# Attention with a relative bias, then a squared-relu layer: v of two batches as fp32 by another queue, x turned by pairs, layer 1 begun with three of four pairs

## The chip, the cores and the metric

The kernel runs on one core of a Trainium2 chip. A core has five engines with their own instruction streams: TensorE (PE, matrix products; its weight loads are shown apart as PEld), VectorE (DVE), ScalarE (ACT), GpSimd (POOL) and SyncE (SP). Sixteen DMA engines move data; they are fed by queues, of which this kernel uses the software queue, issued by GpSimd, and hardware queues, issued by SyncE and ScalarE. The metric is device time in microseconds of one execution.

## The reference

For 8 batches, 8 heads, 576 positions and 64 channels it computes an attention whose bias depends on the distance alone, and puts the result, as 4608 tokens of 512 channels, through two layers with a squared relu between them:

```python
scores = scale * np.matmul(q, k.transpose(0, 1, 3, 2))
bias = bias_table[bucket]                     # bucket of |i - j|, constant from 128 on
attn = softmax(scores + bias.transpose(2, 0, 1)[None])
x = (attn @ v) -> [4608, 512]
h = np.maximum(x @ w_in, 0.0)                 # w_in [512, 2048]
out = h * h @ w_out                           # w_out [2048, 512]
```

All inputs and the output are fp32.

## The kernel before

Products run in fp16. The attention is cut into 32 pairs of heads (four to a batch). `load_six` and `load_rows` bring q and k of a pair into staging tiles `qs`, `ks`, `load_v_head`, `load_v` and `load_v_tail` bring v into `va` (keys 0 to 511) and `vm` (the last 64 keys). All these go by the software queue, which changes fp32 to fp16 on the way; only pair 0's q and k come as fp32 through SyncE's and ScalarE's queues, into a part of a tile `g` that layer 1 uses much later, and are cast by `cast_first` (L463 to L472).

`pair` does one pair. TensorE turns q and k (L608; batches 0 to 2, later batches by DMA), their evacuation L570 (ScalarE) or L572 (VectorE) gives `qt` and `kt`, and L635 spreads the last 64 rows into `qz`. L653 forms the scores of 128 keys for both heads, L702 those of the last keys, L677 those of the last queries. ScalarE takes exponentials of them into `pt` and `pm` (L664, L712, L687). The bias is a factor, exp(bias) from a table `tb_sb` (made by L353 and L365/L367, `tm_sb` by L374), that VectorE multiplies onto the band where it isn't constant (L745). Then L781 and L788 multiply by v in two parts, of three and of two tiles of 128 queries, into the one bank `pv`; a column of constants in v makes the sums, and L805 and L810 divide by them and write `x`.

`x_turn` (batches 0 to 2) is called once for a batch: for each of five tiles of queries it turns the four pairs' x by TensorE (L848) and copies the result into `xt`. Later batches do it by DMA (L826).

`layers` works on groups of 512 tokens: sixteen pieces of layer 1, each of four products of 512 columns (L1044), a relu (L1065 on ScalarE, L1067 on VectorE for the first groups), a square (L1075), and the pieces of layer 2 of the group before, in `second` (L962), which computes with seven products of halves in place of eight (L921 forms sums for it).

PSUM has two score banks pairs `st`, one bank `pv` and three banks `f` that all else shares.

Nothing of this is issued in the order of the text. `P.add` records each piece with its engines, an assumed duration, what it depends on, the buffers it uses, a due time and an earliest time; `Plan.schedule` places the pieces in a simulated order: each engine takes what can begin first, then what is due first. The instructions are then emitted in that order, and each engine executes its own in order. So an assumed duration or a due time changes the order of instructions, and nothing else. The constants at the top (L31 to L41) set due times: `LEAD`, `FAST` and `PERIOD` those of the pairs, `AHEAD` how early a pair may start, `G0` and `GP` those of the groups of layers, `ORDER` the sequence of loads, `QUIET` and `LATER` earliest times of the constant fills (L388), `EV` up to which pair evacuations are VectorE's alone.

The software queue's loads of v of batch 0 are issued after those of pairs 1 to 3 and one of w_in.

Of the kernel before, what the change touches and what calls it, by code (L numbers as in the profile page):

```python
# [25 lines left out]
GT = 512  # L26
# [4 lines left out]
PERIOD, LEAD, FAST, FASTN = 9600.0, 1600.0, 3000, 7  # L31
AHEAD, G0, GP = 20600.0, 54700.0, 35900.0
DT_X = 3
RELU_DVE = 2
NSTG, NQK, NPT, NV, NX, NGB, NRT, NY = 5, 4, 3, 3, 6, 2, 4, 4
QUIET, LATER = 5200.0, 8500.0
TAB, EV = 6400.0, 1
P_ORDER = "1 6 2 5 7 3 4"
P_LAST = "1 6 2 5 7 3 4"
SIX = 3  # L40
ORDER = "k0 i0 q0 q1 v i1 i2 o0 k1 o1 i3 o2 o3"  # L41
# [149 lines left out]
def kernel(  # L191
# [74 lines left out]
    def loader(eng_name, eng, out_, in_, packets, deps=(), bufs=(), due=0.0):  # L266

        lane = [Buf(r_lane)] if eng_name == "POOL" else []
        issue = P.add(
            {eng_name: 720.0 if eng_name == "POOL" else 600.0},  # L270
            lambda: io(eng.dma_start(out=out_(), in_=in_())),  # L271
            deps,
            list(bufs) + lane,
            due,
        )
        return P.add({"DMA": packets / 16}, None, [issue], list(bufs) + lane, due if lane else -1e9), issue
# [9 lines left out]
    def load(eng_name, eng, out_, in_, packets, deps=(), bufs=(), due=0.0):  # L286
        return loader(eng_name, eng, out_, in_, packets, deps, bufs, due)[0]
# [15 lines left out]
        128 * 27, due=0,  # L303
# [21 lines left out]
        {"PE": 250.0},  # L325
# [21 lines left out]
    for c in range(6):  # L347
# [11 lines left out]
        o = P.add({"PE": 16 * 55.0}, t_mm, [o_eb, l_oh], [t_b], LEAD + TAB, 0.0, "f")  # L359
# [27 lines left out]
    def fill(ap, value, ns, due, after, deps=()):  # L387
# [3 lines left out]
    z_fix = [[fill(zz[:, 0], 0.0, 150.0, 10, QUIET)], [fill(zz[:, 1:], 0.0, 300.0, 11, LATER)]]  # L391
    first = [
        fill(pt_sb[:, :, PW:], 1.0, 150.0, 20, LATER),
        fill(pm_sb[:, :, S:], 1.0, 150.0, 20, LATER),
# [11 lines left out]
        fill(stg[i][w][96:128, 512:640].bitcast(FP32), 0.0, 90.0, 40 + i, 25000.0)  # L406
# [56 lines left out]
    def cast_first(w):  # L463

        def cast(o):
            src, dst = first_f[0:96, ts(w, 768)], stg[b_stg[0].slot][w][0:96, :]
            if o.eng == "ACT":
                io(nc.scalar.activation(out=dst, in_=src, func=COPYF))
            else:
                io(nc.vector.tensor_copy(out=dst, in_=src))  # L470

        l_qk[0, w] = [one_of({"ACT": act(768), "DVE": dve(768, 2.0)}, cast, [l_first[w]], [b_stg[0]], -3.0)]  # L472

    def load_v_head(b, h):
        l = load(
            "POOL", nc.gpsimd,
            lambda: vas[b_v[b].slot][:, :, h, 0:64],
            const(v[b, h, 0:512, :].rearrange("(t p) d -> p t d", p=128)),
            512 * 34.5, v_fix[min(b, 1)], [b_v[b]], pdue(),
        )  # L480
        l_v.setdefault((b, h // 2), []).append(l)
# [12 lines left out]
    def load_v(b):  # L494
# [9 lines left out]
        load_v_tail(b)  # L504

# [22 lines left out]
    for hp in range(4):  # L528
# [5 lines left out]
        if hp == 2:  # L534
            load_v_tail(0)
        if hp >= 1:
            for h in range(2 * hp - 2, 2 * hp):
                load_v_head(0, h)
    for h in range(6, 8):
        load_v_head(0, h)  # L540
    for step in ORDER.split():
# [7 lines left out]
        else:  # L549
            load_v(1)  # L550
# [11 lines left out]
    xt_ready, x_last = {}, {}  # L562
# [17 lines left out]
    def pair(p):  # L580
# [5 lines left out]
        for w, dst in ((0, qts), (1, kts)):  # L586
# [14 lines left out]
            def tr(w=w, bank=bank):  # L601
                ps = g_ps[bank.slot].bitcast(FP16)
                t = stg[b_stg[p].slot][w]
                if b < SIX:
# [11 lines left out]

            o = P.add({"PE": 12 * 36.0 if b < SIX else 5 * mm(128)}, tr, l_qk[p, w] + [l_id], [bank, b_stg[p]], T - 3000, after, "c" if b < SIX else "f")

# [152 lines left out]
        for part, qt0, nq in ((0, 0, 3), (1, 3, 2)):  # L771
            bank = Buf(r_pv)

            def pv(qt0=qt0, nq=nq, bank=bank):
                ps = pv_ps[bank.slot][:, 0 : nq * 130].rearrange("p (t e d) -> p t e d", t=nq, e=2)
# [27 lines left out]
            def recip(nq=nq, bank=bank, rb=rb):  # L803
                ps = pv_ps[bank.slot][:, 0 : nq * 130].rearrange("p (t e d) -> p t e d", t=nq, e=2)
                io(nc.vector.reciprocal(out=rs[rb.slot][:, 0:nq], in_=ps[:, :, :, 64:65]))  # L805

            def norm(nq=nq, bank=bank, rb=rb, qt0=qt0):
# [289 lines left out]
    for b in range(B):  # L1097
        norms = [pair(4 * b + hp) for hp in range(4)]
        if b < DT_X:
            x_turn(b, norms)  # L1100
# [38 lines left out]
```

The softmax here doesn't subtract the row's maximum and nothing guards it: scores larger than these inputs give would overflow.

## Time and profile before

| | |
|---|---|
| time, median of 13 runs | 377.3 us (375.82 to 378.54) |
| the profiled execution | 377.51 us, its span 375.7 us |
| mean granted TensorE clock | 0.995 |
| busy: PE, DVE, ACT, POOL | 361.0, 268.8, 255.4, 178.8 us |
| software queue | 94496 packets, 18.07 MB, 62.7% of 16 engines' span |
| hardware queues of loads, stores and transposes | 51280 packets, 19.75 MB, 25.9% |
| first pv product; first product of layer 1 | 20.47 us; 40.65 us |

A profile is of one execution. Its span goes from the first to the last instruction; the execution's time also has what lies around it. Busy time of TensorE counts from a product's start to its modelled end, so that a busy TensorE is not one at its peak. A wait is put down to the engine whose event came last.

### The profile page before, as it was taken

How to read it: one execution, taken by the hardware profiler on the slowest of the kernel's cores; microseconds unless marked ns; L12 is line 12 of the kernel's file. 1: busy time of each engine (PE TensorE's matmuls, PEld its weight loads, DVE VectorE, ACT ScalarE, POOL GpSimd, SP SyncE). 2: the span in 40 equal slices, each digit the busy share in tenths (PEclk: the TensorE clock that was granted, in tenths of full speed). 3: DMA queues.
4: the chain of work that ended last, by engine and by line, in shares of the span. 5: the costliest groups of instructions: out<-in, count | busy, mean ns of one | idle time of the engine just before them, and what ended most of it. 6: DMA issues, size and time to landing. Idle time of an engine off the chain costs nothing.

```text
span 375.7 us, 10050 instructions
## 1 busy us (share of the span) xinstructions
PE 361.0 (96%) x4046; PEld 247.4 (66%) x4046; DVE 268.8 (72%) x612; ACT 255.4 (68%) x361; POOL 178.8 (48%) x318
## 2 busy tenths in 40 slices
PE   3888999999999999999999999999999999999996
PEld 2665546745778666687766765677577888556775
DVE  3987789998788586767685777757776683583653
ACT  4988889987667886866787778746885541564330
POOL 8877453889476582933768456754550000000000
PEclk9989999999999999999999999999999999999999
DMA  9999999799999799949999699899990222100103
GB/s 172 150 131 155 200 167 80 47 92 86 101 152 138 93 120 139 109 52 122 138 132 71 107 124 160 76 105 107 160 108 30 77 58 71 67 2 28 58 28 112
DMA packets 146163, 38.74 MB, mean 103 GB/s; under 512 B 128070, under 2 KB 146118, under 8 KB 146118
## 3 DMA queue, kind: packets, MB, share of 16 engines
q0 software_dynamic: 94496, 18.07, 62.7%
q1 hardware_dynamic: 51280, 19.75, 25.9%
q8 instruction: 31, 0.51, 0.6%
q10 hardware_dynamic: 342, 0.30, 0.3%
q14 instruction: 14, 0.11, 0.1%
HBM read 36.88 MB, written 9.44 MB: 123 GB/s over the span
## 4 chain that ended last, share of the span: by engine, by line
PE 90%; DVE 4%; ACT 3%; DMA 1%; issue 1%; ACTq 0%
PE f L1044 34%; PE f L962 29%; PE pv L788 10%; PE st L653 8%; PE pv L781 3%; PE st L702 2%; PE f L608 1%; PE st L677 1%; DMA g<-in_k_dram 1%; ACT pt L664 1%; ACT pt L687 1%; PE f L848 1%; DVE tb_sb L367 1%; DVE pt L745 1%; DVE kt L572 0%
## 5 line engine op out<-in xcount | busy, mean ns | idle before, releaser
L1044 PE MATMUL f<-xt,w_in_sb 128*128 128x512 f16 (+4 forms) x704 | 142.1, 341 | 0.0
L664 ACT ACTIVATE pt<-st 128x1024 f16<-128x1024 f32 x128 | 126.7, 1023 | 22.4 <-PE st L653 22.4
L1065 ACT ACTIVATE rt<-f 128x512 f16<-128x512 f32 x134 | 80.0, 598 | 62.0 <-PE f L1044 60.3
L1044 PEld LDWEIGHTS <-w_in_sb 128*128 128x128 f16 x704 | 62.6, 98 | 53.0 <-issue 10.8
L1075 DVE TENSOR_TENSOR g<-rt 128x512 f16<-128x512 f16 x144 | 60.6, 423 | 41.2 <-ACT rt L1065 40.1
L745 DVE TENSOR_TENSOR pt<-pt,tb_sb 128x1536 f16<-128x1536 f16 (+2 forms) x96 | 58.3, 622 | 10.4 <-ACT pt L664 10.1
L962 PEld LDWEIGHTS <-g 128*128 128x128 f16 x576 | 54.9, 98 | 15.4 <-issue 4.7
L788 PE MATMUL pv<-va,pt 128*128 128x65 f16 x1280 | 55.5, 194 | 0.1
L788 PEld LDWEIGHTS <-pt 128*128 128x128 f16 x1280 | 51.0, 98 | 3.1 <-issue 0.7
L271 POOL DMA_DIRECT2D qs<-in_q_dram x71 | 49.8, 719 | 2.0 <-DMA ks<-in_k_dram 0.9
L271 POOL DMA_DIRECT2D ks<-in_k_dram x71 | 50.0, 713 | 1.4 <-DMA kt<-ks 0.8
L962 PEld LDWEIGHTS <-s 128*128 128x128 f16 x432 | 40.6, 98 | 10.6 <-issue 3.4
L635 POOL COPY qz<-qt 64x64 f16<-64x64 f16 x53 | 15.6, 294 | 61.9 <-DMA qt<-qs 39.0
L989 DVE SCALAR_TENSOR_TENSOR y<-f,y 128x512 f32<-128x512 f32 (+1 forms) x47 | 31.3, 667 | 16.1 <-PE f L962 15.1
L653 PE MATMUL st<-qt,kt 64*128 64x512 f16 x256 | 40.4, 385 | 1.5 <-ACT pt L664 0.5
L635 POOL COPY qz<-kt 64x64 f16<-64x64 f16 x59 | 20.7, 351 | 36.3 <-DMA kt<-ks 22.9
L962 PE MATMUL f<-w_out_sb,s 128*128 128x256 f16 x288 | 36.6, 273 | 0.0
L962 PE MATMUL f<-wt,g 128*128 128x256 f16 x288 | 36.6, 273 | 0.0
L962 PE MATMUL f<-w_out_sb,g 128*128 128x256 f16 x288 | 36.2, 273 | 0.1
L781 PE MATMUL pv<-vm,pm 128*128 128x130 f16 x160 | 35.5, 222 | 0.5 <-DVE x L810 0.4
L810 DVE TENSOR_TENSOR x<-pv,r 128x384 f16<-128x384 f32 x64 | 31.3, 490 | 1.9
L271 POOL DMA_DIRECT2D va<-in_v_dram x36 | 30.8, 860 | 0.4 <-issue 0.2
(62 smaller groups left out, 306.8 us busy)
## 6 DMA issues: line engine op xcount, KB each, us to landing
out_dram<-y SPq DMA_DIRECT2D x34, 256.0 KB, 2.4
va<-in_v_dram POOLq DMA_DIRECT2D x28, 128.0 KB, 4.7
qs<-in_q_dram POOLq DMA_DIRECT2D x40, 64.0 KB, 3.3
ks<-in_k_dram POOLq DMA_DIRECT2D x40, 64.0 KB, 2.8
w_in_sb<-in_moe_w_in_dram POOLq DMA_DIRECT2D x4, 512.0 KB, 7.5
w_out_sb<-in_moe_w_out_dram POOLq DMA_DIRECT2D x4, 512.0 KB, 9.8
qs<-in_q_dram POOLq DMA_DIRECT2D x11, 144.0 KB, 5.1
ks<-in_k_dram POOLq DMA_DIRECT2D x11, 144.0 KB, 5.9
```

What stands on the lines that cost most here:

```text
L271: lambda: io(eng.dma_start(out=out_(), in_=in_())),
L635: io(eng.tensor_copy(out=dst[qb.slot][rw, rw], in_=src[qb.slot][rw, 512:576]))
L653: nc.tensor.matmul(sets_ps[st.slot][:, e, :], kt[rw, ts(jt, 128)], qt[rw, 0:512], start=True, stop=True,)
L664: nc.scalar.activation(out=p5(pts[pb.slot])[:, jt, :, 0:512], in_=sets_ps[st.slot], func=EXPF, scale=SCALE)
L745: io(nc.vector.tensor_tensor(out=a, in0=a, in1=t, op=MULT))
L781: nc.tensor.matmul(ps[:, i, :, :], pm[:, c : c + 128], vm[:, hp, :, 0:65], start=True, stop=False)
L788: nc.tensor.matmul(ps[:, i, e, :], pt[:, (2 * jt + e) * S + c : (2 * jt + e) * S + c + 128], va[:, jt, 2 * hp + e, 0:65], start=False, sto ...
L810: nc.vector.tensor_tensor(out=xs[xb.slot][:, qt0 : qt0 + nq, :].rearrange("p t (e d) -> p t e d", e=2), in0=ps[:, :, :, 0:64], in1=rs[rb.s ...
L962: nc.tensor.matmul(g_ps[bf.slot][:, ts(s_, HALF)], left(c, s_), right(c), start=(c == 0 and (s_ == 0 or apart) and i not in before), stop= ...
L1044: nc.tensor.matmul(g_ps[bank.slot][:, a:z], w_in_sb[:, kk, ts(nt, 128)], xt_sb[:, kk, c : c + z - a], start=(kk == 0), stop=(kk == 3),)
L1065: io(nc.scalar.activation(out=rts[rb.slot], in_=g_ps[bank.slot], func=RELUF))
L1075: nc.vector.tensor_tensor(out=gs[gb1.slot][:, nt, :], in0=rts[rb.slot], in1=rts[rb.slot], op=MULT)
```

## The change

v of batches 0 and 1 is fetched by `fetch_v` as fp32, six DMAs each on SyncE's queue, into the free part of the last `g` tile (`room_f`, used by batch 0 and then by batch 1), and GpSimd casts it into `va` and `vm`, six casts each. The software queue's loads with an order number above 6, which is all after those of pairs 1 to 3, are made dependent on the first two casts (`v_cast[0:GATE]`). Layer 1 of the group that writes that `g` tile waits for all casts.

Pair 0's q and k are cast into an order in which six transposes of 128 rows do what twelve of 64 did. For batch 0 the second part of pv goes to a bank `f` instead of `pv`. `x_turn` is called for a pair, not a batch: three and two transposes, each with one copy. In the first group, three pieces of layer 1 (`PRE`) are split: the products of three pairs first, and that of pair 3 after. Relus of three groups, not two, may be VectorE's.

Assumed durations and the constants change too, and with them the order on every engine. The constant fills get early earliest times, and evacuations of pairs 1 to 4 become VectorE's alone.

```diff
-PERIOD, LEAD, FAST, FASTN = 9600.0, 1600.0, 3000, 7
-AHEAD, G0, GP = 20600.0, 54700.0, 35900.0
+PERIOD, LEAD, FAST, FASTN = 9200.0, 1800.0, 3000, 8
+AHEAD, G0, GP = 25000, 51600.0, 44700.0
-RELU_DVE = 2
+RELU_DVE = 3
-QUIET, LATER = 5200.0, 8500.0
-TAB, EV = 6400.0, 1
-P_ORDER = "1 6 2 5 7 3 4"
+QUIET, LATER = 1300.0, 900.0
+TAB, EV = 7800.0, 5
+P_ORDER = "1 2 6 5 7 3 4"
-ORDER = "k0 i0 q0 q1 v i1 i2 o0 k1 o1 i3 o2 o3"
+PV_G, PRE, FILL = 1, 3, 0
+V0_AT, V1_AT, V1_LAT, GATE = 3000.0, 15000.0, 12000.0, 2
+ORDER = "i0 q0 k0 k1 q1 i1 o0 i2 o1 o2 i3 o3"
...
+        if eng_name == "POOL" and due > 6.0:
+            deps = list(deps) + v_cast[0:GATE]
...
-        fill(stg[i][w][96:128, 512:640].bitcast(FP32), 0.0, 90.0, 40 + i, 25000.0)
+        fill(stg[i][w][96:128, 512:640].bitcast(FP32), 0.0, 90.0, 40 + i, FILL)
...
-            src, dst = first_f[0:96, ts(w, 768)], stg[b_stg[0].slot][w][0:96, :]
+            src = first_f[0:96, ts(w, 768)].rearrange("p (e j d) -> p e j d", e=2, j=6)
+            dst = stg[b_stg[0].slot][w][0:96, :].rearrange("p (j e d) -> p e j d", e=2, j=6)
...
+    room_f = gs[NGB - 1].bitcast(FP32).rearrange("p t c -> p (t c)")[:, 1536:]
+    r_room = Ring(1)
+    def fetch_v(b):
+        rb = Buf(r_room)
+        for tt in range(4):
+            l = load(
+                "SP", nc.sync,
+                const(room_f[:, ts(tt, 512)].rearrange("p (h d) -> p h d", h=H)),
+                const(v[b, :, ts(tt, 128), :].transpose([1, 0, 2])),
+                1024 * 19, (), [rb], -0.5 + b, after=(V0_AT, V1_AT)[b], turn=6.5 + 3 * b,
+            )
+            o = P.add(
+                {"POOL": 780.0},
+                lambda tt=tt: io(
+                    nc.gpsimd.tensor_copy(
+                        out=vas[b_v[b].slot][:, tt, :, 0:64],
+                        in_=room_f[:, ts(tt, 512)].rearrange("p (h d) -> p h d", h=H),
+                    )
+                ),
+                [l] + v_fix[min(b, 1)], [rb, b_v[b]], -1.0, (0.0, V1_AT + V1_LAT)[b],
+            )
+            v_cast.append(o)
+            for hp in range(4):
+                l_v.setdefault((b, hp), []).append(o)
...
-        if hp == 2:
-            load_v_tail(0)
-        if hp >= 1:
-            for h in range(2 * hp - 2, 2 * hp):
-                load_v_head(0, h)
-    for h in range(6, 8):
-        load_v_head(0, h)
+    fetch_v(0)
+    fetch_v(1)
...
+                if p == 0:
+                    for j in range(6):
+                        io(nc.tensor.transpose(ps[:, ts(j, 96)], t[0:96, ts(j, 128)], id_sb[0:96, 0:96]))
...
-            bank = Buf(r_pv)
+            bank, home = (Buf(r_g), g_ps) if b == 0 and part and PV_G else (Buf(r_pv), pv_ps)
...
+        for part, qt0, nq in ((0, 0, 3), (1, 3, 2)):
             bank = Buf(r_g)
+            n = min(128 * nq, S - 128 * qt0)
...
+                for i in range(nq):
+                    io(nc.tensor.transpose(ps[:, ts(i, 128)], xs[xb.slot][:, qt0 + i, :], id_sb))
...
+                ahead = 3 if g == 0 and i < PRE else 0
+                o = None
+                if ahead:
+                    o = P.add(
+                        {"PE": ahead * mm(512)}, lambda f1=f1: f1(k1=3),
+                        [x for kk in range(ahead) for x in xt_pair[g, kk]] + [l_win[nt // 4]], [bank, gb1],
+                        due + i * 2000, 0.0, "f",
+                    )
...
+                    [o] + (v_cast if g == NGB - 1 else []) + xt_ready[g] + [l_win[nt // 4]], [bank, gb1], due + i * 2000, 0.0, "f"
...
+        for p in range(4 * b, 4 * b + 4):
+            norms = pair(p)
+            if b < DT_X:
+                x_turn(p, norms)
```

## The prediction

> **What bounds the kernel now.** I read the page's busy shares first, then busy time by stretches of 10 us, then the waits of TensorE, then the chain that ended last inside the first 45 us. From the page:
>
> ```profile
> PE 361.0 (96%) x4046; PEld 247.4 (66%) x4046; DVE 268.8 (72%) x612; ACT 255.4 (68%) x361; POOL 178.8 (48%) x318
> ```
>
> Busy time by stretch (PE, PE's weight loads, DVE, ACT, POOL, then the granted clock and DMA):
>
> ```profile
> 0.00:10.00 10.00, 4.12 (x66) 3.03 (x66) 3.96 (x17) 4.75 (x7) 8.19 (x17) 1.00 0.96 174
> 10.00:20.00 10.00, 8.15 (x166) 5.53 (x161) 9.64 (x26) 9.51 (x13) 9.26 (x17) 1.00 1.55 150
> 20.00:30.00 10.00, 9.42 (x180) 7.19 (x178) 8.19 (x29) 8.66 (x13) 7.41 (x14) 0.83 1.27 107
> 30.00:40.00 10.00, 7.82 (x142) 5.63 (x137) 7.09 (x19) 8.46 (x14) 7.33 (x14) 1.00 1.21 190
> 40.00:50.00 10.00, 10.00 (x109) 4.89 (x107) 7.21 (x16) 8.52 (x11) 1.48 (x3) 1.00 1.24 203
> ```
>
> From 40 us on TensorE is full; its idle time lies in the first 40 us (10.5 us, of which 5.9 is the wait for the first k), 0.4 at 361 us and 3 us at the end. So nothing but the first 40 us can give time back; later, only the amount of TensorE work and its order count. The waits of TensorE name the opening one:
>
> ```profile
> PE f L608 <- DVE ks L470: 5.9, 1, 5.9
> ```
>
> The chain inside the first 45 us (start, length, what) then goes over VectorE until the first attention product:
>
> ```profile
> 5.88 1.19 PE f L608 x24
> ...
> 9.11 0.38 DVE qz L388
> 9.48 0.21 DVE pt L388
> 9.69 0.21 DVE pm L388
> 9.90 0.06 issue
> 9.96 0.50 DVE vm L388
> 10.46 0.14 DVE va L388
> ...
> 20.80 0.39 PE pv L788 x7
> ```
>
> The memsets of L388 stand on it for 1.5 us, and first pv waits for the bands of pair 0. By 1-us stretches TensorE's granted clock is 0.50 to 0.71 from 21 to 25 us, after a stretch (18 to 20) in which it was 47% busy; pieces of eight pv products take 0.39 there and 0.24 at 28 us. From 32.6 to 37.2 TensorE waits for ScalarE (0.85, 0.32 and 0.36 us), and the last turn of x waits 0.57 us for its normalisation:
>
> ```profile
> 33.81 0.40 PE L702 MATMUL st<-qt,qz 128*128 128x288 f16 x2 [0.85 <-ACT pt L664]
> ...
> 39.72 0.45 PE L848 MATMUL f<-id_sb,x 128*128 128x128 f16 x5 [0.57 <-DVE x L810]
> ...
> 40.65 2.76 PE L1044 MATMUL f<-xt,w_in_sb 128*128 128x512 f16 x12
> ```
>
> **What the Trainium skill says.** "TensorE: Matmul & The Clock Gate", Part 1, has the array at half clock until it has been busy for a window of some 3.4 us, and again after too little work; the 0.50 at 22 us agrees. "DMA: Bandwidth & Descriptors", Queues, rings and completion order: each DMA engine takes packets in turn from the queues that have work, so a second queue takes share from the first; this trace has only the software queue loaded early, so no line shows it. "SBUF — State Buffer", Who interferes with whom: VectorE in its two-port modes and GpSimd lock each other out; GpSimd's 64x64 copies take 0.23 us at 7 to 13 us and 0.29 to 0.35 on average, which fits without proving it.
>
> **The change, part by part.** Instruction counts are from the two programs' orders, durations from the trace.
>
> *Opening.* Pair 0's 24 transposes (two halves each) become 12 of full width. 24 took 1.19 us, so 0.6 us less on the chain: -0.6. The cast before them writes strided; I keep its 0.56 us (if its rate halved, +0.4).
>
> *Memsets.* The fills, 3.1 us in sum with the ten staging ones at 25.6 us, now stand ahead of the first cast, where VectorE is idle from 1.0 to 5.27 us. They fit with 1 us to spare; were they not covered, each would delay the first cast. Off the chain: -1.5.
>
> *VectorE or ScalarE.* Before the first pv VectorE has two more evacuations of 128x576 (2 x 0.75) and six fewer qz copies (6 x 0.2, now GpSimd's): +0.3. Up to the first relu VectorE has, in all, 12 such evacuations instead of 7 (+3.75), four more qz copies (+0.9), two more pm bands (+0.5), more but smaller x copies (+0.3), less the memsets: about 3 us more than before, against 6.3 us that it was idle between 5 and 40. ScalarE has 18 exponentials instead of 20 (-2.06), one more each of L712 and L687 (+1.26), three evacuations fewer (-2.0): -2.8. TensorE has the same work up to there (about 22 us by columns in both, at the rate of the 56 products that take 12.09 us from 323 us on). ScalarE's relief goes against the 1.5 us that TensorE waited for it at 33 to 37: -1.2. Of VectorE's remaining 2.7 us extra, most falls in its idle time; 1.0 comes through: +1.0 (bounds 0 and 2.7).
>
> *x by pairs, layer 1 with three pairs.* Only the last pair's five transposes are left at the end, and three groups can start without pair 3. Before, the closing stretch 37.55 to 40.65 held 20 transposes with a wait of 0.57: -0.9 (bounds 0 and -1.5). The second pv part goes to another bank; its wait on the normalisation was only 0.4 us in all; counted as nothing.
>
> *v.* Eight 64 KB, four 128 KB and four 32 KB loads leave the software queue: GpSimd saves 16 issues of 0.63 to 0.86 us and gains twelve casts. A cast of 128x512 is not in the trace. Bounds: 0.23 us (a 64-wide copy's price) and 8 x 0.23 = 1.84; I take 0.8, near one element a cycle plus a fixed part, and 0.5 for the tails. Casts of batch 0 follow the qz copies, so from about 13 us: 4 x 0.8 + 2 x 0.5 + two load issues (1.4) + a qz copy = 5.9, done at 19. The first pv needs all six and came at 20.5, so they are hidden; at 1.84 they would end at 24 and cost 3.5. Queued behind them are the loads of pair 4's and later q and k, w_in and w_out. Pair 4's q is issued between the casts at about 16 and lands 5 us later, wanted at about 23. The casts of batch 1 hold back the third and fourth w_in until about 33 us; those land by some 49 (7.5 us each, in turn), wanted from 48 on: hidden with little left. On SP's queue nothing stands behind the v loads until the transposes of batch 3. The v packets are now, by an estimate from the queues' averages, 30.4 ns each (25.9% x 16 x 375.7 us over 51280 on the hardware queue) instead of 39.9 (62.7% over 94496): 9216 packets, 5.5 us less DMA time; not on the path by itself. But batch 0's 4608 packets, 8.8 us of all engines, now run beside the q and k of pairs 1 to 3. I take +0.3 (bounds 0 and +4).
>
> *Later.* After layer 1 begins TensorE goes through 392 runs of one kind instead of 368. Ten are x turns between other work, the rest mostly f1 and f2 by turns. A run of eight f2 products took 0.98 us after another kind and 0.87 after f1, so a turn costs up to 0.11 on each side: 10 x 0.08 on average: +0.8 (bounds 0 and 2.6). Relus of the third group may go to VectorE, which was 94 to 97% busy from 60 to 90 us; it is spread over more time, so nothing.
>
> Sum: -0.6 - 1.5 + 0.3 - 1.2 + 1.0 - 0.9 + 0.3 + 0.8 = -1.8. Profiled span 375.7, so 373.9; the profiled execution took 377.51, 1.8 more than its span, and the median is 377.3, 1.6 above the span. Forecast 375.5.
>
> **Rivals.** *Absorbed:* VectorE becomes the bound of the opening. With 30.6 us of work from 5.3 and its old 5 to 6 us of idle time it lets layer 1 begin at 41, as before; the start's gain is gone, the turns stay, memsets help: 376.9. For it: VectorE 96% busy from 10 to 20. Against: part of its idle time was waiting for ScalarE.
>
> *Slower:* v's packets take half of the DMA engines while pairs 2 and 3 load. The last of the six loads, issued at 4.55, landed about 6 us later; at half rate the 4.3 us (0.86 MB at 200 GB/s) that were left from 4.2 us on become 8.6, so it lands near 15. In the new order pair 3's q is turned ahead of pair 0's last score, at about 12 us. From that point each microsecond of lateness stops TensorE in order, 3 us, and its clock falls again, 1 us more: -1.8 - 0.3 + 4 = +1.9, so 379.2. Against: only the first two v loads are issued at once; the other four wait for SP's earlier transfers and start near 5 us.
>
> *More:* the clock doesn't drop at 21 us, since transposes and tables fill 16 to 20: another 1.8 us, and VectorE's extra is all hidden, 1.0: 372.7.
>
> **How the numbers follow.** Forecast 0.50 (own range 373.7 to 376.5), absorbed 0.20, slower 0.20, more 0.10. A change within 0.2% (376.5 to 378.1) can hardly be told from none. Faster: 0.50 + 0.10 + a tenth of absorbed, 0.62; same: most of absorbed, 0.17; slower: 0.20 and a tail of absorbed, 0.21. The range 372.0 to 379.0 leaves out about the upper half of the slower case and the lower half of the larger gain.
>
> **What would show it.** Right: memsets before 5.2 us and none after; first layer-1 product at 38 to 40 us (40.65 before); no TensorE wait over 0.3 us on ScalarE there; the casts on GpSimd under 1 us and over before the first pv. Wrong: TensorE waiting on a q or k load between 9 and 17 us; the first pv released by GpSimd; VectorE busy over 95% from 20 to 40 us with layer 1 at 41 or later; layer 1's third quarter waiting for w_in; more TensorE idle time past 50 us.

## The result and the profile after

The changed kernel takes 381.43 us (median of 11 runs, 379.77 to 384.96) against 377.37 (48 runs, 375.82 to 379.18) on the same chips: ratio 1.0128 [1.0108, 1.0149]. It is 4.1 us slower; I forecast 1.8 us faster. The eleven times fall into two groups, six from 379.77 to 381.43 us and five from 383.67 to 384.96, and the median is the edge of the lower one. The profiled execution took 385.19 us, just above the upper group, with a span of 383.4 and a clock of 0.991, so its sums below are larger than the median's loss, and no trace shows an execution of the lower group.

Busy shares, from the page of the kernel after:

```profile
PE 363.4 (95%) x4034; PEld 247.1 (64%) x4034; DVE 276.2 (72%) x628; ACT 250.2 (65%) x354; POOL 171.5 (45%) x314
```

Of the 7.7 us between the two spans, 5.3 are idle time of TensorE (383.4 - 363.4 = 20.0 against 375.7 - 361.0 = 14.7), and 2.4 are TensorE busy for longer, with twelve products fewer. The stretches of 10 us after show where (same columns as for before: PE, PEld, DVE, ACT, POOL, clock, DMA share, GB/s), and then the last of them before:

```profile
20.00:30.00 10.00, 8.13 (x156) 5.72 (x154) 8.97 (x25) 7.84 (x10) 6.41 (x11) 1.00 1.27 203
30.00:40.00 10.00, 9.03 (x194) 6.52 (x191) 9.11 (x28) 9.57 (x17) 2.35 (x5) 1.00 0.81 131
40.00:50.00 10.00, 5.50 (x19) 2.11 (x21) 3.43 (x10) 2.29 (x5) 7.35 (x15) 0.68 1.02 157
...
70.00:80.00 10.00, 8.45 (x182) 6.87 (x178) 9.80 (x25) 9.08 (x14) 8.17 (x21) 1.00 0.45 30
```

```profile
70.00:80.00 10.00, 9.85 (x121) 5.80 (x117) 9.68 (x24) 9.53 (x16) 8.62 (x17) 1.00 0.75 54
```

From 40 to 50 us, where TensorE had been full, it is idle for 4.5 us and then runs at a lower clock; and from 70 to 80, where before had 9.85, it is idle for 1.5 us while VectorE is 98% busy (97% before). GpSimd, 2.35 us busy in the stretch ahead, is the odd one. The waits of TensorE after name it:

```profile
PE f L648 <- DVE ks L478: 5.9, 1, 5.9
PE st L750 <- POOL qz L683: 4.4, 1, 4.4
```

The first is the wait for the first k, as before; the second is new. TensorE's timeline after shows what it does (start, length, what, and in brackets the idle time before and who ended it):

```profile
40.12 0.81 PE L1090 MATMUL f<-xt,w_in_sb 128*128 128x512 f16 x3
45.31 0.66 PE L750 MATMUL st<-qt,qz 128*128 128x288 f16 x2 [4.37 <-POOL qz L683]
45.76 0.63 PE L725 MATMUL st<-qz,kt 128*128 128x128 f16 x4
46.19 3.62 PE L1090 MATMUL f<-xt,w_in_sb 128*128 128x512 f16 x8
```

Layer 1 begins at 40.12 us, 0.5 earlier than before, and after three products TensorE stands at a score that needs a `qz`. Eight products of layer 1 then take 3.62 us; eight took 1.90 in the kernel before, at 43.88 us. The Trainium skill, "TensorE: Matmul & The Clock Gate", Part 1, has half clock again after too little work; twice 1.90 is 3.80, so this agrees, with a mean clock of 0.68 in this stretch. GpSimd's timeline after says why `qz` was late:

```profile
29.74 0.63 POOL L520 CAST va<-g 128x512 f16<-128x512 f32 x1 [1.79 <-DMA g<-in_v_dram]
35.65 0.62 POOL L520 CAST va<-g 128x512 f16<-128x512 f32 x1 [5.29 <-DMA g<-in_v_dram]
37.47 0.40 POOL L544 CAST vm<-g 64x256 f16<-64x256 f32 x1 [1.21 <-DMA g<-in_v_dram]
38.97 0.40 POOL L544 CAST vm<-g 64x256 f16<-64x256 f32 x1 [1.10 <-DMA g<-in_v_dram]
39.42 0.74 POOL L277 DMA_DIRECT2D w_in_sb<-in_moe_w_in_dram  x1
40.15 1.49 POOL L277 DMA_DIRECT2D w_out_sb<-in_moe_w_out_dram  x2
...
44.45 0.51 POOL L683 COPY qz<-qt 64x64 f16<-64x64 f16 x2
```

It stood for 9.4 us (1.79 + 5.29 + 1.21 + 1.10) at the casts of batch 1, each waiting for its own load; behind them were seven issues of loads, and only then the copies. The chain that ended last (start, length, what) goes back over the load to SyncE's queue:

```profile
18.67 0.41 POOL vm L544
19.09 6.86 SPq L277
...
26.04 12.81 DMA g<-in_v_dram
...
38.97 0.40 POOL vm L544
...
44.45 0.23 POOL qz L683
...
45.31 0.66 PE st L750 x2
```

Batch 1's v uses the same room as batch 0's, so each of its loads waits for the cast that empties its part. That delays them little: the first four were issued at 14.77, 15.75, 17.09 and 18.30 us, each right behind such a cast. What is late is their landing. The third and fourth ended the waits at 29.74 and 35.65 us above, so they landed more than 12 and 17 us after their issue. The fifth issue then held SyncE for 7 us, and the last load, issued behind it, took 12.81 us more. SyncE's timeline after, in short windows:

```profile
18.30 0.50 SPq L277 DMA_DIRECT2D g<-in_v_dram  x1
18.89 7.06 SPq L277 DMA_DIRECT2D g<-in_v_dram  x1
26.04 1.13 SPq L277 DMA_DIRECT2D g<-in_v_dram  x1
```

The page's list of DMA issues after (KB each, median us from issue to landing):

```profile
va<-in_v_dram POOLq DMA_DIRECT2D x24, 128.0 KB, 4.7
...
g<-in_v_dram SPq DMA_DIRECT2D x8, 256.0 KB, 9.6
w_in_sb<-in_moe_w_in_dram POOLq DMA_DIRECT2D x4, 512.0 KB, 9.2
w_out_sb<-in_moe_w_out_dram POOLq DMA_DIRECT2D x4, 512.0 KB, 11.3
```

The w loads, 7.5 and 9.8 us before, are slower too. The Trainium skill, "DMA: Bandwidth & Descriptors", Queues, rings and completion order, has each DMA engine take packets in turn from the queues that have work. That fits the slow landings of v, but no run isolates it: of the eight w loads only three were issued while v was still on its way, the other five from 39.42 us on.

### The profile page after: what moved, and what is told of

Read it like the earlier page. It is cut to its first block, busy times and chain, and to the rows that moved or that the text cites. A ratio compares the mean times of both kernels' runs of the same rounds, so it can differ in the third digit from the quotient of the medians.

```text
span 383.4 us, 10056 instructions
## 1 busy us (share of the span) xinstructions
PE 363.4 (95%) x4034; PEld 247.1 (64%) x4034; DVE 276.2 (72%) x628; ACT 250.2 (65%) x354; POOL 171.5 (45%) x314
## 4 chain that ended last, share of the span: by engine, by line
PE 86%; DMA 5%; DVE 4%; POOL 3%; SPq 2%; issue 1%; ACT 0%; POOLq 0%
PE f L1090 33%; PE f L1008 29%; PE pv L836 8%; PE st L701 8%; DMA g<-in_v_dram 3%; PE pv L829 2%; SPq L277 2%; PE st L750 2%; PE st L725 1%; DMA g<-in_k_dram 1%; DVE s L967 1%; DVE pt L793 1%; PE f L653 1%; PE f L899 1%; POOL va L520 1%
## 5 line engine op out<-in xcount | busy, mean ns | idle before, releaser
L1090 PE MATMUL f<-xt,w_in_sb 128*128 128x512 f16 (+4 forms) x704 | 144.7, 344 | 0.1
L1120 ACT ACTIVATE rt<-f 128x512 f16<-128x512 f32 x129 | 76.9, 598 | 70.0 <-PE f L1090 68.3
L793 DVE TENSOR_TENSOR pt<-pt,tb_sb 128x512 f16<-128x512 f16 (+2 forms) x96 | 58.2, 622 | 9.5 <-ACT pt L712 9.4
L836 PE MATMUL pv<-va,pt 128*128 128x65 f16 x1216 | 51.9, 193 | 0.4 <-DVE pt L793 0.4
L836 PEld LDWEIGHTS <-pt 128*128 128x128 f16 x1280 | 50.1, 97 | 3.3 <-issue 1.2
L683 POOL COPY qz<-qt 64x64 f16<-64x64 f16 x58 | 17.8, 307 | 53.6 <-DMA qt<-qs 32.9
L829 PE MATMUL pv<-vm,pm 128*128 128x130 f16 x152 | 33.6, 221 | 1.0 <-DVE x L858 1.0
L683 POOL COPY qz<-kt 64x64 f16<-64x64 f16 x54 | 16.2, 299 | 35.2 <-DMA kt<-ks 24.5
L858 DVE TENSOR_TENSOR x<-pv,r 128x384 f16<-128x384 f32 (+1 forms) x60 | 29.7, 495 | 2.0
L760 ACT ACTIVATE pm<-st 128x576 f16<-128x576 f32 x32 | 20.9, 655 | 9.1 <-PE st L725 5.9
```

Of the source, the lines that this page charges most:

```text
L683: io(eng.tensor_copy(out=dst[qb.slot][rw, rw], in_=src[qb.slot][rw, 512:576]))
L793: io(nc.vector.tensor_tensor(out=a, in0=a, in1=t, op=MULT))
L829: nc.tensor.matmul(ps[:, i, :, :], pm[:, c : c + 128], vm[:, hp, :, 0:65], start=True, stop=False)
L836: nc.tensor.matmul(ps[:, i, e, :], pt[:, (2 * jt + e) * S + c : (2 * jt + e) * S + c + 128], va[:, jt, 2 * hp + e, 0:65], start=False, sto ...
L1090: nc.tensor.matmul(g_ps[bank.slot][:, a:z], w_in_sb[:, kk, ts(nt, 128)], xt_sb[:, kk, c : c + z - a], start=(kk == 0), stop=(kk == 3),)
L1120: io(nc.scalar.activation(out=rts[rb.slot], in_=g_ps[bank.slot], func=RELUF))
```

## The experiments

Every edit of a load, a cost or a due time makes the planner write a new order on all engines from that place on. It can do more than the section on the kernel before says: where a piece may go to one of two engines (`one_of`), the planner chooses the engine too, so an assumed duration or a due time also moves pieces between engines. "TensorE 0-40" and "40-80" are its busy time in those stretches of each profiled execution; "layer 1" is its first product; where three pieces are split, this is the first of three products of three pairs.

| kernel | us (median) | ratio to before, 95% | layer 1 at | TensorE 0-40 | 40-80 |
|---|---|---|---|---|---|
| before | 377.4 | | 40.65 | 29.51 | 39.74 |
| after | 381.43 | 1.0128 [1.0108, 1.0149] | 40.12 | 30.31 | 33.59 |
| v1_cast_late | 379.44 | 1.0057 [1.0035, 1.0079] | 40.14 | 30.86 | 38.09 |
| v1_soft | 379.32 | 1.0044 [1.0028, 1.0061] | 41.14 | 31.26 | 37.57 |
| qz_vector | 379.73 | 1.0056 [1.0030, 1.0081] | 41.69 | 28.98 | 38.10 |
| v_soft | 379.60 | 1.0056 [1.0036, 1.0076] | 35.10 | 31.76 | 36.79 |
| v_only | 383.20 | 1.0173 [1.0130, 1.0216] | 41.64 | 28.78 | 37.37 |
| lat_sums_later | 378.11 | 1.0022 [1.0006, 1.0039] | 40.51 | 31.32 | 38.27 |
| lat_old_times | 380.54 | 1.0084 [1.0051, 1.0116] | 41.31 | 30.53 | 37.44 |
| lat_x_by_batch | 379.63 | 1.0074 [1.0042, 1.0106] | 40.00 | 30.64 | 37.32 |
| fills_early | 379.13 | 1.0049 [1.0026, 1.0072] | 38.31 | 29.85 | 37.55 |
| x_pairs_alone | 379.46 | 1.0046 [1.0031, 1.0062] | 37.67 | 30.50 | 37.85 |
| soft_sums_later | 378.35 | 1.0017 [1.0001, 1.0032] | 34.25 | 31.02 | 37.83 |
| order_only_early | 381.05 | 1.0087 [1.0063, 1.0110] | 41.73 | 30.28 | 37.22 |
| order_only_products | 378.89 | 1.0039 [1.0025, 1.0053] | 40.63 | 29.48 | 39.89 |

Theory A was that batch 1's late v, through the casts and the `qz` copies behind them, makes the loss; its rival B that VectorE is the bound anyway, with or without the stop. C to H were formed later, and are stated with the runs.

**Is the stop at 41 us due to batch 1's casts?** In v1_cast_late only the time from which the planner may place those casts is later.

```diff
-V0_AT, V1_AT, V1_LAT, GATE = 3000.0, 15000.0, 12000.0, 2
+V0_AT, V1_AT, V1_LAT, GATE = 3000.0, 15000.0, 26000.0, 2
```

> Edit: the six casts of batch 1's v stand later in GpSimd's order (their earliest time 14 us later), behind the third and fourth w_in, the other w_out and the qz copies of pairs 4 to 7; all else of the changed kernel is kept. Theory A (the casts wait for v loads that land late, and the qz copies queued behind them stop TensorE for 4.4 us, after which its clock is halved): that wait goes, the time falls by 4 to 6 us to 375.5 to 377.5. Rival B (VectorE bounds the opening and 66 to 78 us): the wait is only moved, TensorE waits for VectorE instead, 380 to 382. Rival C (the loads of w_in that are late hold layer 1): also better, as they come forward too, but the qz wait stays.

In v1_soft batch 1's v comes by the software queue, as in the kernel before, in place of `fetch_v(1)`.

```diff
-ORDER = "i0 q0 k0 k1 q1 i1 o0 i2 o1 o2 i3 o3"
+ORDER = "i0 q0 k0 k1 q1 v i1 o0 i2 o1 o2 i3 o3"
...
-    fetch_v(1)
```

> Edit: batch 1's v by the software queue as before the change, batch 0's v still fp32 by SyncE's queue. Theory A: no cast of batch 1 is left to hold GpSimd, so no wait of TensorE for GpSimd; 375.5 to 377.5, as with the later casts. Rival B: 380 to 382, since VectorE's work is as much as in the changed kernel.

In qz_vector the loads and casts stay, and the copies into `qz` of three pairs may not be GpSimd's.

```diff
-                spread.append(one_of({"DVE": 200.0, "POOL": 320.0} if b < DT_QK else {"POOL": 320.0}, sp, [evac[w]] + z_fix[min(p, 1)], [qb], T - 1000))
+                spread.append(one_of({"DVE": 200.0} if b < DT_QK and p in (5, 6, 7) else {"DVE": 200.0, "POOL": 320.0} if b < DT_QK else {"POOL": 320.0}, sp, [evac[w]] + z_fix[min(p, 1)], [qb], T - 1000))
```

> The whole change, with the qz copies of pairs 5, 6 and 7 on VectorE and not left to the planner, so that none of them stands behind the second batch's casts on GpSimd. Theory A (TensorE's stop at 41 us is the qz copies queued behind the waiting casts): no wait of TensorE for qz there, no halved clock from 41 to 50, and about 379 to 380.5. Rival A2 (TensorE would have stopped there anyway for the w_in loads that stand behind the same casts): the wait turns into one for w_in_sb, and the time stays at 381 to 384.

All three take the stop away and come out alike: 379.44, 379.32 and 379.73 us, 1.7 to 2.1 less than the whole change's median. In v1_cast_late the four casts of 128x512 run back to back at 41 us, with no wait; its timeline of GpSimd, and then its stretch from 40 to 50 us:

```profile
41.21 2.47 POOL L520 CAST va<-g 128x512 f16<-128x512 f32 x4
```

```profile
40.00:50.00 10.00, 10.00 (x77) 4.58 (x76) 9.72 (x21) 7.66 (x11) 6.52 (x14) 1.00 1.24 206
```

qz_vector decides between the two things queued behind the casts. There GpSimd still stands 5.00 us at a cast, and issues the third w_in as late as 38.08 us:

```profile
34.12 0.61 POOL L520 CAST va<-g 128x512 f16<-128x512 f32 x1 [5.00 <-DMA g<-in_v_dram]
...
38.08 0.74 POOL L277 DMA_DIRECT2D w_in_sb<-in_moe_w_in_dram  x1
```

yet TensorE is busy for 9.87 of the 10 us from 40 to 50 at full clock:

```profile
40.00:50.00 10.00, 9.87 (x87) 4.73 (x86) 9.42 (x25) 8.15 (x14) 4.95 (x8) 1.00 1.14 181
```

So the late w_in alone stops nothing, and the `qz` copies did. Theory A is right on the mechanism; its time of 375.5 to 377.5 for the first two is not reached, nor is Rival B's of 380 to 382. In part B's other forecast came true: with the stop gone TensorE is still idle for 1.9 to 2.4 us from 40 to 80, where before had 0.26. About 2 us of the loss have another source. The trace of v1_cast_late shows little of them: its execution took 378.20 us, the second fastest of nine (378.07 to 380.94), and its span is 0.7 us above that of before.

**v on its own.** v_soft keeps all other parts and gives v of both batches back to the software queue; v_only is the kernel before with `fetch_v` for both batches and the two-cast gate, and nothing else.

```diff
-ORDER = "i0 q0 k0 k1 q1 i1 o0 i2 o1 o2 i3 o3"
+ORDER = "i0 q0 k0 k1 q1 v i1 o0 i2 o1 o2 i3 o3"
...
-    fetch_v(0)
-    fetch_v(1)
+    load_v_tail(0)
+    for h in range(8):
+        load_v_head(0, h)
```

And v_only:

```diff
-ORDER = "k0 i0 q0 q1 v i1 i2 o0 k1 o1 i3 o2 o3"
+V0_AT, V1_AT, V1_LAT, GATE = 3000.0, 15000.0, 12000.0, 2
+ORDER = "k0 i0 q0 q1 i1 i2 o0 k1 o1 i3 o2 o3"
...
+        if eng_name == "POOL" and due > 6.0:
+            deps = list(deps) + v_cast[0:GATE]
...
-        if hp == 2:
-            load_v_tail(0)
-        if hp >= 1:
-            for h in range(2 * hp - 2, 2 * hp):
-                load_v_head(0, h)
-    for h in range(6, 8):
-        load_v_head(0, h)
+    fetch_v(0)
+    fetch_v(1)
```

> Edit: v of both batches by the software queue, all other parts of the change kept. Theory A: 376 to 379, batch 0's loads in the software queue cost some DMA time back. Rival B (the parts other than v cost the time): 380 or more.

> Edit: the kernel before with nothing changed but v of both batches as fp32 by SyncE's queue, GpSimd's casts and the two-cast gate. Theory A: slower than before by 2 to 6 us, with GpSimd waiting for late v loads between 25 and 40 us and qz copies behind its casts. Rival B: within 1 us of before.

v_only is 5.8 us slower than before, at the top of what A allowed. The waits of TensorE in it show the same stop, and q and k loads that land late beside v:

```profile
PE st L750 <- POOL qz L683: 2.5, 1, 2.5
PE pv L829 <- DVE x L858: 1.8, 4, 0.8
...
PE f L656 <- DMA ks<-in_k_dram: 1.1, 2, 0.7
```

v_soft begins layer 1 at 35.10 us, 5.5 earlier than before, and is still 2.2 us slower. The table shows how: by 40 us TensorE has done 2.25 us more than before, and from 40 to 80 2.95 less. Its 379.60 us lie between the forecasts of Theory A (376 to 379) and Rival B (380 or more). By 40 us it has also done 1.45 us more than the whole change, and v_only less than before (28.78 against 29.51), so fetching v by SyncE's queue seems to hold up the opening too.

**Which of the other parts takes the 2 us?** First each alone, in the kernel before: the early fills (with the change's assumed durations for them), and the turns of x by pairs (`x_turn` itself as in the change).

```diff
-QUIET, LATER = 5200.0, 8500.0
+QUIET, LATER, FILL = 5200.0, 900.0, 0
...
-        fill(stg[i][w][96:128, 512:640].bitcast(FP32), 0.0, 90.0, 40 + i, 25000.0)
+        fill(stg[i][w][96:128, 512:640].bitcast(FP32), 0.0, 90.0, 40 + i, FILL)
```

> The kernel before with nothing but the memsets moved ahead of the first cast. The forecast put 1.5 us on them: 375.5 to 376.3 if this part was right. Rival: the first pv waits for the loads and bands of pair 0 anyway, so 377 to 377.8, no change.

```diff
-        norms = [pair(4 * b + hp) for hp in range(4)]
-        if b < DT_X:
-            x_turn(b, norms)
+        for p in range(4 * b, 4 * b + 4):
+            norms = pair(p)
+            if b < DT_X:
+                x_turn(p, norms)
```

> The kernel before with nothing but the turns of x by pairs (ten turns of three or two transposes for each batch of the first three, and no layer-1 group begun with three pairs). The forecast: -0.9 for the closing stretch and +0.8 for more turns between kinds of work, so 377 to 377.6. Rival F (the turns by pairs cost in the 60 to 80 us stretch, where VectorE is late: more and smaller copies): 378.5 to 380.

Both do what they were forecast to do for the opening, and more: layer 1 begins at 38.31 and 37.67 us. Both are slower, by 1.8 and 2.1 us; no forecast for fills_early allowed that, and x_pairs_alone is in Rival F's range. Then two put back, in v1_cast_late: the constants of the times, and (in lat_sums_later, which follows) x by batch, with `x_turn` as before and no group begun with three pairs.

```diff
-PERIOD, LEAD, FAST, FASTN = 9200.0, 1800.0, 3000, 8
-AHEAD, G0, GP = 25000, 51600.0, 44700.0
+PERIOD, LEAD, FAST, FASTN = 9600.0, 1600.0, 3000, 7
+AHEAD, G0, GP = 20600.0, 54700.0, 35900.0
-RELU_DVE = 3
+RELU_DVE = 2
-P_ORDER = "1 2 6 5 7 3 4"
+P_ORDER = "1 6 2 5 7 3 4"
```

> v1_cast_late with the planner's constants of the kernel before put back (period, lead, due time of layer 1, share of relus open to VectorE, order of the pairs); all built-in parts of the change stay (v by SP, x by pairs, three of four pairs, early memsets). Theory E (the retuning of the times makes layer 1 run dense from 40 to 66 us and so VectorE late): about 377, TensorE over 9 of 10 us from 60 to 80. Rival F (the parts themselves cost, above all x by pairs, and not the times): 379 to 381.

```diff
-PV_G, PRE, FILL = 1, 3, 0
+PV_G, PRE, FILL = 1, 0, 0
...
-        for p in range(4 * b, 4 * b + 4):
-            norms = pair(p)
-            if b < DT_X:
-                x_turn(p, norms)
+        norms = [pair(4 * b + hp) for hp in range(4)]
+        if b < DT_X:
+            x_turn(b, norms)
```

> lat_sums_later (378.1) with x turned by batch as in the kernel before, and no group of layer 1 begun with three pairs. Rival F (turning x by pairs costs about 2 us wherever it stands, as alone: 379.5 against 377.4): 376 to 377. Theory C (any order costs that puts more of VectorE's work between 60 and 80 us, and x by pairs is one of them but not more than others): 377.5 to 379.5.

Neither gives anything back: 380.54 and 379.63. The first, of four runs, is in Rival F's range (379 to 381) and not in Theory E's (about 377); the second is outside F's (376 to 377). So x by pairs costs 2 us alone, and taking it out of the other kernel makes that 1.5 us slower. No part tried has a price that goes with it wherever it stands; Rival F falls.

**Is it VectorE's work?** In most of these profiles TensorE waits between 60 and 80 us for what VectorE writes, and VectorE is 92 to 98% busy (94 and 97% in the two stretches before). lat_sums_later is v1_cast_late, and soft_sums_later v_soft, with the sums of the activations due later, so that VectorE takes them later.

```diff
-                    [gb] + [sb_[i] for i in uses], G0 + GP * g - 5e4,
+                    [gb] + [sb_[i] for i in uses], G0 + GP * g - 1e4,
```

> The run with the second batch's casts moved back (v1_cast_late, 379.4), and on top of it the due time of the sums of the activations 40 us later, so that VectorE takes them after the normalisations between 60 and 78 us and not before. Theory C (what is left of the loss, about 2 us, is VectorE being late there: the relus and sums of the first group come before the normalisations that TensorE waits for): 376.5 to 378.5, and TensorE over 8.8 of 10 us in the stretch 60 to 70 (8.11 in v1_cast_late). Rival D (VectorE has too much work there in any order, or the sums are needed soon anyway): 379 to 380.5, the same waits for x moved by a few us.

> v_soft (379.6) with the sums of the activations due 40 us later, as in lat_sums_later, where this gave 1.3 us; a whole kernel. Theory C: 378 to 378.8, not faster than before, since VectorE has the same work. If only the order mattered: 375 to 377, since layer 1 begins 5 us earlier.

378.11 and 378.35 us, 1.33 and 1.25 less than without, as Theory C forecast: when VectorE does this work matters, or the new order that comes with it. TensorE's stretch from 60 to 70 hardly fills, though (8.37, where C had over 8.8); v1_cast_late first, then lat_sums_later:

```profile
60.00:70.00 10.00, 8.11 (x186) 6.36 (x186) 9.76 (x21) 9.27 (x18) 6.73 (x15) 1.00 0.40 28
```

```profile
60.00:70.00 10.00, 8.37 (x160) 5.32 (x157) 9.40 (x24) 8.37 (x14) 7.15 (x15) 1.00 0.66 43
```

The two profiled executions took 378.20 and 378.02 us, so these traces can't show where the medians part.

For the amount, I gave the eight sums of w_out's parts to GpSimd, in lat_sums_later and in the kernel before.

```diff
-                    {"DVE": dve(1024, 2.0)},
-                    lambda out_=out_, a=a, b_=b_, op=op: io(nc.vector.tensor_tensor(out=out_, in0=a, in1=b_, op=op)),
-                    l + [o], (), 1e5,
+                    {"POOL": 2000.0},
+                    lambda out_=out_, a=a, b_=b_, op=op: io(nc.gpsimd.tensor_tensor(out=out_, in0=a, in1=b_, op=op)),
+                    l + [o], (), 3e4,
```

> lat_sums_later (378.1) with the eight sums of w_out's parts, 8 x 0.69 us, on GpSimd and not on VectorE. Theory C2 (from 60 to 80 us TensorE goes at VectorE's pace, so work taken from VectorE comes back as time): 376 to 377.2, TensorE idle under 1 us from 60 to 80 (1.7 in lat_sums_later). Rival G (the starved stretches come from the order and not from the amount): 377.8 to 379. A third way: GpSimd takes over 2 us for each sum and is late with qz copies or loads behind them: over 379, TensorE waiting for qz.

> The kernel before with the eight sums of w_out's parts on GpSimd and not on VectorE. It has only 0.26 us of TensorE idle time from 60 to 80, so Theory C2 expects no gain, 377 to 378; slower if GpSimd is late with its copies or the new order packs worse, as other small edits did (up to 379.5).

399.88 us (ratio 1.0601 [1.0574, 1.0628]) and 401.02 (1.0629 [1.0591, 1.0666]): the times of both theories are missed, and the third way (over 379, GpSimd late with `qz` copies) has the sign but not the cause. GpSimd was hardly late with copies (one wait of 1.4 us, in wsums_gp_before); VectorE's own operations became long, and TensorE waited for them. GpSimd's and then VectorE's timeline of wsums_gp_lat:

```profile
51.94 2.17 POOL L947 TENSOR_TENSOR wt<-w_out_sb 128x1024 f16<-128x1024 f16 x1
54.06 0.66 POOL L277 DMA_DIRECT2D qs<-in_q_dram  x1
54.74 2.13 POOL L947 TENSOR_TENSOR wt<-w_out_sb,wt 128x1024 f16<-128x1024 f16 x1
```

```profile
52.05 2.34 DVE L1130 TENSOR_TENSOR g<-rt 128x512 f16<-128x512 f16 x1
54.32 4.72 DVE L793 TENSOR_TENSOR pt<-pt,tb_sb 128x640 f16<-128x640 f16 x1
```

A square takes 0.42 us on average elsewhere and a band of 128x640 0.48 (at 28.64 us of the kernel after). So this told nothing on the amount. The next three leave these sums out: the three kinds of products that read them read w_out's own parts, so the output is another.

```diff
-    t_done = sums_of_weights()
+    t_done = l_wout
...
-            6: ("b", lambda c, s: ss[2][:, c, s], lambda c: wt_sb[:, 0, c], [2]),
+            6: ("b", lambda c, s: ss[2][:, c, s], lambda c: w4[:, c, 0, 0], [2]),
```

> v1_cast_late (379.4) without the eight sums of w_out's parts; the three products that read them read w_out's own parts in their place, so TensorE's work is the same and VectorE has 8 x 0.69 = 5.5 us less; what is computed is not the reference. Theory C (TensorE goes at VectorE's pace from 60 to 80 us): 376.5 to 377.8, TensorE idle under 0.7 us from 60 to 80 (1.9 in v1_cast_late). Rival G (the order, not the amount): 378.5 to 380.

> v_soft (379.6), whose layer 1 begins at 35 us, without the eight sums of w_out's parts, as above; what is computed is not the reference. Theory C: the opening's gain now comes through, 374.5 to 377. Rival G: 378.5 to 380.

> The kernel before without the eight sums of w_out's parts, as above; what is computed is not the reference. Its TensorE is idle for only 0.26 us from 60 to 80, so Theory C expects nearly nothing: 376.8 to 377.8. If it falls by 2 us or more, VectorE's amount of work costs in some other way that the idle time of TensorE doesn't show. Rival G: any new order costs, up to 379.5.

379.40 (1.0059 [1.0041, 1.0078]), 379.15 (1.0052 [1.0038, 1.0066]) and 377.38 us (1.0011 [0.9986, 1.0036]): nothing moves by more than 0.5 us. That is Rival G's forecast for the first two. The stretch from 60 to 70 of no_wsums_lat is that of v1_cast_late over again, VectorE included:

```profile
60.00:70.00 10.00, 8.09 (x186) 6.32 (x185) 9.76 (x21) 9.27 (x17) 6.68 (x15) 1.00 0.38 26
70.00:80.00 10.00, 10.00 (x157) 8.12 (x154) 7.37 (x20) 7.99 (x12) 8.50 (x16) 1.00 0.92 77
```

The work went from 70 to 80 us, where TensorE had been full. So in this kernel the experiment took it from the wrong place; in no_wsums_soft VectorE falls from 9.77 to 8.99 of 10 us in the right place, from 60 to 70, and TensorE rises from 8.52 to 9.31, but the median moves by 0.45 us only. The amount of VectorE's work isn't shown as the cause. And no_wsums_before, planned anew as well, loses nothing.

**Or is it a new order?** Two kernels have all operations and loads of the kernel before, but not all on the same engines: the planner moved some. In the second, ScalarE takes four pieces that were VectorE's (three copies of x, one relu); in the first, at least sixteen change their engine, among them three evacuations of q and k from ScalarE to VectorE, and four copies of x and three evacuations of layer 2 the other way. The first has three of the change's assumed durations, the second the change's order of the seven products.

```diff
-        {"PE": 250.0},
+        {"PE": 500.0},
...
-        o = P.add({"PE": 16 * 55.0}, t_mm, [o_eb, l_oh], [t_b], LEAD + TAB, 0.0, "f")
+        o = P.add({"PE": 16 * 33.0}, t_mm, [o_eb, l_oh], [t_b], LEAD + TAB, 0.0, "f")
...
-            o = P.add({"PE": 12 * 36.0 if b < SIX else 5 * mm(128)}, tr, l_qk[p, w] + [l_id], [bank, b_stg[p]], T - 3000, after, "c" if b < SIX else "f")
+            o = P.add({"PE": 12 * 30.0 if b < SIX else 5 * mm(128)}, tr, l_qk[p, w] + [l_id], [bank, b_stg[p]], T - 3000, after, "c" if b < SIX else "f")
```

> The kernel before with three of the durations that the planner assumes changed as in the change (the table's products 33 ns each and not 55, a transpose 30 and not 36, the far product 500 and not 250). No load, no operation and no constant is another; only the order that the planner writes differs, from the first table product on. Theory H (the old order is one that happens to pack without a gap from 40 to 360 us, and most other orders of the same work cost 1 to 2.5 us): 378.4 to 380, TensorE idle 1 us or more from 40 to 80 (0.26 in the kernel before). Rival (parts of the change cost, the order does not): 376.8 to 377.9.

```diff
-P_ORDER = "1 6 2 5 7 3 4"
+P_ORDER = "1 2 6 5 7 3 4"
```

> The kernel before with the change's order of the seven products of layer 2 (1 2 6 5 7 3 4 and not 1 6 2 5 7 3 4), which writes another order from about 70 us on and leaves all work as it is. Theory H: 377.8 to 379.5, gaps of TensorE past 70 us. Rival: 376.8 to 377.9.

381.05 (four runs) and 378.89 us: a new plan of the same operations costs 3.6 and 1.4 us. The three stretches of before, and then of order_only_early:

```profile
0.00:40.00 40.00, 29.51 (x538) 21.38 (x538) 28.89 (x88) 31.38 (x43) 32.19 (x61) 0.96 1.25 155
40.00:80.00 40.00, 39.74 (x490) 22.57 (x486) 35.93 (x83) 36.44 (x54) 22.42 (x41) 1.00 0.99 113
80.00:360.00 280.00, 279.83 (x2917) 193.24 (x2917) 197.14 (x430) 186.16 (x264) 124.19 (x218) 1.00 0.87 96
```

```profile
0.00:40.00 40.00, 30.28 (x532) 21.12 (x533) 29.03 (x86) 30.38 (x41) 31.61 (x60) 0.96 1.20 145
40.00:80.00 40.00, 37.22 (x481) 21.82 (x478) 35.68 (x81) 35.14 (x52) 20.69 (x36) 1.00 0.98 120
80.00:360.00 280.00, 279.33 (x2908) 191.31 (x2906) 196.68 (x428) 186.80 (x267) 125.81 (x223) 1.00 0.85 96
```

Before, TensorE is idle for 0.43 us in the 320 us from 40 to 360 (0.26 + 0.17). In the other order it stops for 2.78 us from 40 to 80, in pieces, those past 60 us of 0.2 to 0.5 each, for VectorE and ScalarE by turns, which are no more busy than before. The gaps are about half of it: over the whole span TensorE is idle for 16.9 us against 14.7, and busy for 363.0 against 361.0 with the same products. In order_only_products, whose order differs from about 70 us on, the gaps lie after 80: 1.61 us up to 360. Theory H's forecasts hold for these two, the first by more than its range. Its wording, that most other orders cost, isn't shown by two, and neither is how much of the cost is the order and how much the engines.

No run is faster than the kernel before.

## Why the prediction was wrong

The step that failed is in the paragraph on v: "The casts of batch 1 hold back the third and fourth w_in until about 33 us ... hidden with little left." It asked which loads stand behind these casts and not which copies, though it had counted `qz` copies as moving to GpSimd two paragraphs earlier. And it gave the casts no wait of their own. Two more sentences fed it: "On SP's queue nothing stands behind the v loads" is true but beside the point, since the v loads stand behind one another (one issue held SyncE for 7.06 us, and the last load was issued at 26.04); and the loads, priced by packets at 5.5 us less DMA time "not on the path by itself", were on it, as those that GpSimd waited for took from 12.6 to 18.5 us from issue to landing. The casts ended at 39.4, not 33. Between medians this step costs 1.7 to 2.1 us, a figure that depends on the median's place at the edge of the lower group; in the profiled execution 4.4 us of wait and about 2 of lower clock. As its own end of range I had named only an effect of batch 0's packets on q and k ("bounds 0 and +4"); that is real but small here (0.5 us of wait for q of one pair).

The second error is of a whole kind: the sum for the opening was carried to the end of the kernel unreduced. "From 40 us on TensorE is full ... later, only the amount of TensorE work and its order count" was right, and then order got +0.8 for turns between products and none for gaps. A plan that leaves 0.43 us idle in 320 has nearly nothing to gain there and much to lose; two other plans of the same operations cost 1.4 and 3.6 us. The remaining 2 us are of that size, and this is argued by likeness. Their cause in the whole change stays open: no part that was tried carries them, and neither VectorE's amount of work nor one due time was shown to.

The opening's own terms failed too. Those up to layer 1 sum to -2.6 us, and it began 0.5 earlier. The first of them, -0.6 for pair 0's transposes, is wrong by itself: the twelve wider ones took nearly as long as the twenty-four (1.19 us), so 0.05 us was saved. From the chain after:

```profile
5.93 1.14 PE f L648 x12
```

By its other steps:

- Memsets: right in place (1.05 to 4.41 us, before the first cast), wrong in worth. Alone they bring layer 1 forward by 2.3 us, and the time is 1.8 longer.
- VectorE and ScalarE: +3.1 us on VectorE up to 40 us (32.03 against 28.89; "about 3 us more"); ScalarE -1.6, where I had -2.8. TensorE's waits for ScalarE at 33 to 37 us are gone, as forecast, but in sum up to 40 us they fell only from 2.6 us to 1.8, where I had -1.2; two of over 0.5 us just ahead of the first pv stayed.
- Casts of batch 0: 0.61 to 0.64 us each (I took 0.8), ended at 19.07 (19), ahead of the first pv at 21.56: hidden, right. That first pv itself came 1.1 us later than before.
- x by pairs: the 60 transposes take 7.3 us busy against 4.9, more than "+0.8", but with the stop gone TensorE's whole busy time is 361.2 against 361.0, so it didn't lengthen the sum. Layer 1 began at 40.12, just past "38 to 40".
- "Relus of the third group ... spread over more time, so nothing": not tested alone; with the old limit put back among the constants (lat_old_times) nothing was gained.
- Rivals: none named the mechanism that decided. "Absorbed" was nearest for the second half, since gains of the opening did vanish, but later than it said and not for VectorE's amount. "Slower" had the right sign, and its place (9 to 17 us) wrong. The premise of "More" came true, a clock of 1.00 from 20 to 30 us, and its gain didn't. That clock isn't of the change's making: order_only_products, planned alike up to about 70 us, has 1.00 there too and begins layer 1 at 40.63, as before, though its first k came 0.5 us later.
- Of the signs of being wrong that I named only one came, more idle time of TensorE past 50 us.

## What to carry to other kernels

When a wait is given to an in-order engine, list everything behind it on that engine, copies as well as DMA issues, and ask of each who stops; the load waited for needs its own start (what frees its buffer, what its queue issues ahead of it) and its landing time under the traffic of that moment. In a kernel whose critical engine has no gaps left after some point, a gain before that point is worth nothing until a run shows it, and any edit that lets a scheduler write a new plan needs a control: the same operations, planned anew. Here that control alone moved the time by 1.4 and 3.6 us, as much as the parts under test. Check in the traces whether the control has kept each piece on its engine; here it had not. And see where a traced execution lies among the times before you read the median's loss from it.

## What the runs showed of the hardware

- GpSimd's tensor operations of 128x1024 fp16 took 2.14 us each in the median, and VectorE's squares and bands of 128x640 beside them took 1.7 to 4.7 us instead of 0.4 to 0.5; with eight sums moved the kernels were 22 to 24 us slower. The Trainium skill, "SBUF — State Buffer", Who interferes with whom, has a VectorE instruction with two SBUF inputs contend with a GpSimd instruction that reads SBUF; this agrees. GpSimd's casts of fp32 to fp16 did it on a smaller scale: beside those of 41.21 to 44.58 us in v1_cast_late two squares took 0.60 and 0.61 us instead of 0.42 and a band of 128x192 0.66 instead of 0.25, while a relu out of PSUM kept its 0.69.

```profile
42.61 0.60 DVE L1130 TENSOR_TENSOR g<-rt 128x512 f16<-128x512 f16 x1
43.13 0.66 DVE L793 TENSOR_TENSOR pm<-pm,tm_sb 128x192 f16<-128x192 f16 x1
```

- The eight 256 KB loads of v by SyncE's queue took 9.6 us in the median from issue to landing, the slowest of all twelve 18.5. The 128 KB loads of v by the software queue took 4.7, but these are the later batches', from 56.9 us on, when no v came by the other queue. One issue on SyncE lasted 7.06 us, where the median of the twelve is 0.60.
- After 4.4 us of waiting TensorE's clock was 0.68 on average from 40 to 50 us, and eight products took 3.62 us.
